# Random-feature attention with a cosine-routed mixture of experts on one core: gate roots and gate work by pairs of token blocks, half sums on TensorE, two GpSimd drains

## Chip, cores and metric

The kernel runs on one core of one Trainium2 chip. The metric is the device time of one execution in microseconds (us); lower is better. TensorE is PE in the profile (PEld is its weight load), VectorE is DVE, ScalarE is ACT, GpSimd is POOL and SyncE is SP; a q behind a name (POOLq, SPq) is the engine's instruction queue.

## The reference, cut to what matters

```python
def phi(x):                                   # omega: 128 x 64
    proj = np.einsum('bhsd,md->bhsm', x, omega)
    return np.concatenate([np.cos(proj), np.sin(proj)], axis=-1) / np.sqrt(m)
q_p, k_p = (phi(q), phi(k))                   # q, k, v: 8 x 8 x 576 x 64
kv = np.einsum('bhsm,bhsd->bhmd', k_p, v)
z = np.sum(k_p, axis=2)
num = np.einsum('bhsm,bhmd->bhsd', q_p, kv)
den = np.einsum('bhsm,bhm->bhs', q_p, z)
...
x = (num / den) as 4608 rows of 512           # 8 heads x 64
xn = x / (np.linalg.norm(x, axis=-1, keepdims=True) + 1e-06)
logits = xn @ en.T / tau                      # en: the 8 normed expert rows
expert_idx = np.argmax(logits, axis=1)
probs = softmax(logits); gate_w = probs[np.arange(N), expert_idx]
for e in range(E):                            # w1: 8 x 512 x 1024, w2: 8 x 1024 x 512
    mask = expert_idx == e
    h = np.maximum(x[mask] @ w1[e], 0.0)
    out[mask] = gate_w[mask, None] * (h @ w2[e])
```

## The kernel before

The work has two stages whose instructions stand in a fixed order written out by hand: each engine runs its own queue in program order, so an instruction that waits holds everything behind it on that engine.

**Attention, 32 steps.** Step n is one pair of heads of one batch (4 pairs, 8 batches; NS is 32). A step projects q and k on TensorE, folds and takes sines and cosines on VectorE and ScalarE, sums the k features on GpSimd (`zsum`, `zsum_tail`, lines 287 to 304), and forms products with v and q on TensorE (lines 312, 333, 348, 379). `norm` divides on VectorE; `to_rows` (GpSimd cast), `sums` (GpSimd, adds a step's unnormed logits to `lacc`) and `squares` (GpSimd, squares the rows in place, line 417; on ScalarE only in the last step) follow one step behind, and `square_sums` (VectorE) three behind. The fp16 rows with their 9 numbers for the gate (8 logits and the sum of squares) go to a buffer in DRAM by SyncE. 32 pieces of expert weights of 512 KB are loaded by GpSimd DMAs, one a step; the set `SOON` (line 1140) says which pieces are issued early in a step, before `norm`, and which at its end.

**Half sums.** The two heads of a step lie in the two halves of the partitions, so a token's logits and sums of squares need both halves added. A group is two batches, and there are four groups. For the logits of the first three and the squares of the first two, ScalarE copies one half beside the other (`other_half`, `square_rows`, line 423) and VectorE adds (`add_halves`, lines 615 and 616, and a reduction at line 443); the rest is added by TensorE matmuls with a stacked identity (`merge`, line 638). The pieces that choose each token's expert are laid into steps 10 to 14 and 18 to 31 (`lay_first`); `rank_here` and `invert_here` are matmuls put after a step's products (`on_pe`).

**Experts, 40 blocks.** Tokens are sorted by expert into blocks of 128; the first 11 blocks (K1) are known before the last attention step, the places of the rest are worked out during blocks 0 to 7 (`route_second`, on VectorE mostly: two comparisons `row_hot` of 128x2304 at line 854, then 36 matmuls `invert` at line 861, then `rows_of_pieces`, which writes the row numbers that gathers 11 to 14 read). Per block j:

- GpSimd gathers the rows of block j+7 (`gather`, line 928, an indirect DMA) into one of four buffers; SyncE turns them (line 977).
- `take_logits` copies the 9 numbers of block j+3 into its slot of `gx` (ScalarE to block 7, VectorE after it), `norm_of` takes the square root on GpSimd as a power (line 449) and adds 1e-6 there (line 450); `gate_shift` (VectorE, lines 984 to 987), `gate_exp` (ScalarE, line 994) and `gate_end` (VectorE, lines 998 and 999) make the gate weight.
- `hidden(j+1)`: 32 matmuls (line 1035), then relu, one half on ScalarE (line 1043), the other on ScalarE to block 7 and on VectorE after it (line 1047). `result(j)`: 8 matmuls (line 1056), the scaled copy on ScalarE (line 1068, below called y(j)), and the scatter to the output by GpSimd (line 1069, an indirect DMA).

In the program's order TensorE does hidden(j+1), then result(j). GpSimd does, for every block from 11 on: square root and addition for block j+3, scatter of block j, gather of block j+7. On VectorE `gate_shift(j+2)` stands ahead of the relu of hidden(j+1). After the 40th block a branch skips three spare blocks, and the kernel ends with drains and semaphores of all engines (lines 1387 and 1431).

Of the kernel before, what the change touches and what calls it, by code (L numbers as in the profile page):

```python
# [11 lines left out]
FP32 = mybir.dt.float32  # L12
# [16 lines left out]
def kernel(  # L29
# [76 lines left out]
    lmax = persist.tile([P, SG], FP32)  # L106
# [23 lines left out]
    pm = persist.tile([P, SG], BF16)  # L130
# [4 lines left out]
    with tc.tile_pool(name="psA", bufs=1, space=PSUM) as psA, tc.tile_pool(  # L135
# [293 lines left out]
        def square_sums(n):  # L429
            b, i = steps[n]  # L430
            if i == 0:
                ssq[b] = pa.tile([P, NCH, 2 * NPAIR], FP32, tag="sq", name="sq", bufs=4)
# [4 lines left out]
        def square_rows(g, par, act):  # L437
            s0 = g * SG
            t = ssq.pop(2 * g + par)
            here = slice(64 * par, 64 * par + 64)  # L440
            there = slice(64 - 64 * par, 128 - 64 * par)
            move("act" if act else "dve", t[here, :, NPAIR:], t[there, :, 0:NPAIR])
            nc.vector.tensor_reduce(
                lsq[here, s0 : s0 + SG, E : E + 1], t[here], axis=AX.X, op=ALU.add
            )
# [140 lines left out]
        def choose_pieces(g, act=True):  # L586
            s0 = g * SG
            lg = lsq[:, s0 : s0 + SG, 0:E]

            def scratch(at, n, own):  # L590
                return ROUTE[:, at : at + n] if act else own

            cp = scratch(0, SG * E, None)
            mx = scratch(72, SG, lmax)
            hit = scratch(81, SG * E, sel.rearrange("p s e -> p (s e)"))
            hit = hit.rearrange("p (s e) -> p s e", e=E)
            top = scratch(153, SG, pm)
            l0, l1 = lg[0:64], lg[64:P]

            def other_half():  # L600
                a0, a1 = lacc[2 * g], lacc[2 * g + 1]
                c0, c1 = l0, l1
                if act:
                    c = cp.rearrange("p (s e) -> p s e", e=E)
                    c0, c1 = c[0:64], c[64:P]
                move("act" if act else "dve", c0, a0[64:P])
                move("act" if act else "dve", c1, a1[0:64])

            def add_halves():
                a0, a1 = lacc.pop(2 * g), lacc.pop(2 * g + 1)  # L610
                c0, c1 = l0, l1
                if act:
                    c = cp.rearrange("p (s e) -> p s e", e=E)
                    c0, c1 = c[0:64], c[64:P]
                nc.vector.tensor_tensor(l0, c0, a0[0:64], ALU.add)
                nc.vector.tensor_tensor(l1, c1, a1[64:P], ALU.add)
# [15 lines left out]
            return [other_half, add_halves, largest, preferred, first_of_them]  # L632

        LATE = ps[:, 6 * 512 + 304 : 7 * 512]

        def merge(at, parts, w):
            for par, t in enumerate(parts):
                nc.tensor.matmul(
                    LATE[64 * par : 64 * par + 64, at : at + w],
                    lhsT=rmat[:, 0, 0, 0:64], rhs=t, start=True, stop=True,  # L640
                )

        def choose_last(g):
            s0 = g * SG
            lg = LATE[:, 0 : SG * E].rearrange("p (s e) -> p s e", e=E)
            nc.scalar.activation(lsq[:, s0 : s0 + SG, 0:E], lg, AF.Copy)
# [500 lines left out]
        for n in range(NS):  # L1147
# [56 lines left out]
            if n > 0:  # L1204
                norm(n - 1)
# [230 lines left out]
```

## Time and profile before

| | us |
|---|---|
| median of 3 runs | 484.4 (482.27 to 495.48) |
| the profiled execution | 485.89 |
| its span, first to last instruction | 484.0 |
| mean granted TensorE clock | 0.986 of full speed |
| last matmul's copy (y of block 39) begins at | 475.12 |

The attention stage takes the first 300 us or so of the span, the expert stage the rest. Rows of the timeline give start, duration, engine, line, operation, what it writes and reads with shapes, a count of merged instructions, and in brackets the idle time before it with what released it.

### The profile page before, as it was taken

What the parts mean: (1) busy time and instruction counts of PE and PEld (TensorE: products, weight loads), DVE (VectorE), ACT (ScalarE), POOL (GpSimd) and SP (SyncE); (2) the same over time, 40 slices, a digit from 0 to 9 for tenths busy, and PEclk for the clock granted to TensorE, in tenths of its full rate; (3) what the DMA queues carried; (4) which work ended last, traced back from release to release, by engine and by line L of the source; (5) the groups of instructions that cost most, each with busy time, mean ns of one, the idle gap of its engine ahead of it and who ended that gap; (6) DMA issues with size and microseconds to landing.
All of it is one profiled execution on the core that took longest, in us unless ns stands there. A gap on an engine that the chain in (4) does not pass through costs nothing. (4 is left out here: it accounts for less than half of the span.)

```text
span 484.0 us, 18932 instructions
## 1 busy us (share of the span) xinstructions
PE 441.2 (91%) x7872; PEld 361.0 (75%) x7872; DVE 321.9 (67%) x731; ACT 342.1 (71%) x457; POOL 389.5 (80%) x500
## 2 busy tenths in 40 slices
PE   5799999999999999988998998799789999999992
PEld 4698988888888888877887887676566666666671
DVE  3589888888888788887898879377643333333340
ACT  6899999999999899887997988455333333333341
POOL 3589999989999889887997979978867777777761
PEclk9999999999999999999999999899899999999997
DMA  6577898888888878957888786447264454454431
GB/s 150 148 157 158 194 165 185 182 178 169 175 182 168 202 156 172 196 127 151 168 184 167 150 177 105 91 115 121 86 128 117 133 128 119 125 139 118 127 96 35
DMA packets 77637, 70.78 MB, mean 146 GB/s; under 512 B 49381, under 2 KB 57573, under 8 KB 77552
## 3 DMA queue, kind: packets, MB, share of 16 engines
q0 software_dynamic: 17920, 31.11, 34.6%
q1 hardware_dynamic: 59328, 38.36, 31.7%
q8 instruction: 65, 1.06, 0.9%
q14 instruction: 20, 0.16, 0.1%
q10 hardware_dynamic: 304, 0.08, 0.1%
HBM read 67.67 MB, written 15.37 MB: 172 GB/s over the span
## 5 line engine op out<-in xcount | busy, mean ns | idle before, releaser
L296 POOL TENSOR_TENSOR zs<-sck 128x512 f32<-128x512 f32 x64 | 82.0, 1282 | 31.2 <-ACT sck L286 28.2
L1056 PE MATMUL ps<-w_sb,late 128*128 x320 | 81.0, 384 | 8.3 <-DVE omT L998 8.3
L1035 PEld LDWEIGHTS <-w_sb 128*128 x1280 | 75.7, 99 | 10.0 <-issue 1.3
L1035 PE MATMUL ps<-kq,w_sb 128*128 128x128 f16 x1280 | 79.2, 221 | 0.7 <-ACT kq L423 0.5
L379 PE MATMUL ps<-kv,siq 128*64 128x73 f32 x1152 | 76.7, 229 | 3.0 <-DVE kv L361 2.8
L379 PE MATMUL ps<-kv,coq 128*64 128x73 f32 x1152 | 75.4, 227 | 0.0
L379 PEld LDWEIGHTS ps<-kv,siq 128*64 128x64 f32 x1152 | 63.5, 136 | 7.5 <-issue 3.3
L379 PEld LDWEIGHTS ps<-kv,coq 128*64 128x64 f32 x1152 | 64.2, 137 | 0.0
L1056 PEld LDWEIGHTS <-late 128*128 128x128 f16 x320 | 29.8, 98 | 42.3 <-DVE late L1047 18.1
L269 DVE SCALAR_TENSOR_TENSOR sck<-sck,ps 128x1152 f32<-128x1152 f32 x32 | 43.3, 1353 | 21.6 <-ACT sck L265 21.6
L985 DVE RECIPROCAL omT<-omT 128x1 f32<-128x1 f32 (+1 forms) x38 | 6.2, 163 | 76.4 <-POOL omT L450 76.4
L221 PEld LDWEIGHTS ps<-omT,kqT 64*128 64x128 f32 x576 | 44.1, 192 | 15.0 <-issue 13.9
L928 POOL DMA_INDIRECT xin_all<-rf_x,prm x40 | 42.7, 1068 | 13.6 <-issue 12.9
L298 POOL TENSOR_TENSOR zs<-zs 128x256 f32<-128x256 f32 x64 | 47.2, 738 | 5.0
L221 PE MATMUL ps<-omT,kqT 64*128 64x128 f32 x576 | 48.6, 282 | 0.6 <-DVE kqT L202 0.6
L276 ACT ACTIVATE sck<-sck 128x1152 f32<-128x1152 f32 x32 | 37.3, 1166 | 12.0 <-DVE sck L269 12.0
L269 DVE SCALAR_TENSOR_TENSOR siq<-siq,ps 128x1152 f32<-128x1152 f32 x32 | 43.0, 1344 | 2.9 <-ACT siq L265 2.9
L280 DVE TENSOR_REDUCE coq<-siq 128x1152 f32<-128x1152 f32 x32 | 43.2, 1350 | 0.1
L184 PE MATMUL ps<-ident,kq 128*128 128x128 f32 x288 | 39.4, 281 | 4.1 <-DVE siq L269 1.7
L265 ACT ACTIVATE siq<-ps 128x1152 f32<-128x1152 f32 x32 | 36.1, 1127 | 9.4 <-PE ps L247 8.3
L312 PE MATMUL ps<-sck,v 64*64 64x128 f32 x1224 | 37.8, 272 | 5.4 <-issue 4.4
L286 ACT ACTIVATE coq<-coq,pio 128x1152 f32<-128x1152 f32 x32 | 39.9, 1248 | 2.5 <-DVE coq L280 2.4
(200 smaller groups left out, 982.6 us busy)
## 6 DMA issues: line engine op xcount, KB each, us to landing
w_sb<-in_moe_w_dram POOLq DMA_DIRECT2D x32, 512.0 KB, 7.4
kq<-in_k_dram SPq DMA_DIRECT2D x64, 144.0 KB, 3.7
kq<-in_q_dram SPq DMA_DIRECT2D x64, 144.0 KB, 3.6
v<-in_v_dram SPq DMA_DIRECT2D x34, 144.0 KB, 4.1
rf_x<-xb SPq DMA_DIRECT2D x32, 144.0 KB, 6.7
xin_all<-in_v_dram SPq DMA_DIRECT2D x30, 144.0 KB, 3.7
xin_all<-rf_x,prm POOLq DMA_INDIRECT x40, 3.4
kq<-xin_all SPq DMA_TRANSPOSE x37, 3.3
```

The costliest lines, as they stand in the source:

```text
L184: nc.tensor.transpose(qreg[:, at : at + P], t[:, j * P : j * P + P], ident)
L221: nc.tensor.matmul(kreg[:, s * P : s * P + P], lhsT=t[r0 : r0 + 64, j * P : j * P + P], rhs=omT[r0 : r0 + 64], start=True, stop=True,)
L269: nc.vector.scalar_tensor_tensor(out=si, in0=si, scalar=CMAGIC, in1=REG[nm], op0=ALU.subtract, op1=ALU.subtract)
L280: nc.vector.tensor_reduce(co.unsqueeze(2), si.unsqueeze(2), axis=AX.X, op=ALU.max, apply_absolute_value=True)
L286: nc.scalar.activation(t, t, AF.Sin, bias=pio2 if which == "co" else 0.0, scale=-TWO_PI * SINSC)
L296: nc.gpsimd.tensor_tensor(z[:, 0:4], t[:, 0:4], t[:, 4:8], ALU.add)
L298: nc.gpsimd.tensor_tensor(r, z[:, 0:2], z[:, 2:4], ALU.add)
L312: nc.tensor.matmul(kreg[64 * half : 64 * half + 64, 512 * hh : 512 * hh + P], lhsT=d["v"][r0 : r0 + 64, c], rhs=d["sck"][r0 : r0 + 64, hal ...
L379: nc.tensor.matmul(nm2[r0 : r0 + 64, a, (c - c0) * W : (c - c0) * W + W], lhsT=ph[:, s * P + r0 : s * P + r0 + 64], rhs=d["kv"][:, half, h ...
L928: ins = nc.gpsimd.indirect_dma_start(out=t, out_offset=None, in_=x_rows[:], in_offset=bass.IndirectOffsetOnAxis(ap=prm[:, j : j + 1], axis=0),
L1035: nc.tensor.matmul(h_ps[:, f * P : f * P + P], lhsT=weights(k), rhs=d["xT"][:, c * P : c * P + P], start=(c == 0), stop=(c == 3),)
L1056: nc.tensor.matmul(y_ps, lhsT=d["hT"][:, c * P : c * P + P], rhs=weights(NW1 + c), start=(c == 0), stop=(c == NW2 - 1),)
```

## The change

- `norm_of` takes the power for two blocks in one GpSimd instruction; the addition of 1e-6 moves into `gate_shift` on VectorE. `gx` has 8 slots, so `take_logits`, `gate_shift` and `gate_end` go by pairs of blocks: logits at even j, `gate_shift` and the exponentials at odd j, `gate_end` at even j. In `route_second` the third block product moves from j = 5 to 4, the two `row_hot` from 6 and 7 to 5 and 6, and `block_experts` behind the gathers.
- All four groups add their half sums by TensorE matmuls; the copies and additions on ScalarE and VectorE go, and one ScalarE copy of 128x72 a group (`kept`) is new.
- Weight pieces 21 and 31 are issued at the end of a step. Gather 0 moves from step 29 to step 30, gathers 1 to 4 stand in step 31 (before: one in step 30, three in 31). The squares of step 29 are taken by ScalarE in step 31.
- `nc.gpsimd.drain()` stands before `result(34)` and `result(37)`.

```diff
         def squares(n):
             x = st[n]["xa"][:, 0:NCH, 0:64]
-            if n < NS - 1:
+            if n not in (NS - 3, NS - 1):
                 nc.gpsimd.tensor_tensor(x, x, x, ALU.mult)
...
+        def gate_slots(j, n=1):
+            a = (j + 1) % 8
+            assert a + n <= 8
+            return gx[:, a : a + n]
 
         def norm_of(j, n=1):
-            r = gx[:, j % 4 : j % 4 + n, E]
+            r = gate_slots(j, n)[:, :, E]
             nc.gpsimd.tensor_tensor(r, r, half1.to_broadcast([P, n]), ALU.pow)
-            nc.gpsimd.tensor_scalar(r, r, 1e-6, None, ALU.add)
...
+        def merge(out, parts):
+            w = out.shape[1]
+            for par, t in enumerate(parts):
+                nc.tensor.matmul(
+                    out[64 * par : 64 * par + 64, 0:w],
+                    lhsT=rmat[:, 0, 0, 0:64], rhs=t, start=True, stop=True,
+                )
...
+            def to_pe():
+                merge_logits(g, at)
+                merge_squares(g, sn)
...
+            def kept():
+                nc.scalar.activation(lsq[:, s0 : s0 + SG, 0:E], lg, AF.Copy)
...
         def gate_shift(j, n=1):
-            g = gx[:, j % 4 : j % 4 + n]
-            nc.vector.tensor_reduce(g[:, :, 10:11], g[:, :, 0:E], axis=AX.X, op=ALU.max)
-            nc.vector.reciprocal(g[:, :, 11], g[:, :, E])
+            g = gate_slots(j, n)
+            nc.vector.tensor_reduce(g[:, :, 9:10], g[:, :, 0:E], axis=AX.X, op=ALU.max)
+            nc.vector.tensor_scalar(g[:, :, E], g[:, :, E], 1e-6, None, ALU.add)
+            nc.vector.reciprocal(g[:, :, 10], g[:, :, E])
...
-            lay(n + 11, [lambda: [piece() for piece in first_rows(r1, K1)], swap], [add])
-            lay(n + 12, [lambda: block_experts(0, K1, False, ar1)], [big])
-            lay(n + 13, [pre], [one])
+            on_pe[n + 10] = lambda: (invert_here(), to_pe2())
+            lay(n + 11, [lambda: [piece() for piece in first_rows(r1, K1)]], [big])
+            lay(n + 12, [], [pre, sq])
+            lay(n + 13, [kept], [one, lambda: block_experts(0, K1, False, Arena(ROUTE[:, 200:]))])
...
-        SOON = {1, 2, 4, 6, 8, 10, 12, 14, 15, 16, 17, 19, 21, 23, 25, 27, 29, 30, 31}
+        SOON = {1, 2, 4, 6, 8, 10, 12, 14, 15, 16, 17, 19, 23, 25, 27, 29, 30}
...
+            if n == NS - 1:
+                squares(n - 2)
...
+            if n == NS - 2:
+                gather(0)
...
-            if NS - 3 <= n < NS:
-                gather(n + 3 - NS)
             if n == NS - 1:
-                gather(3)
-                gather(4)
-            if n > 0:
+                for j in range(1, 5):
+                    gather(j)
+            if n > 0 and n != NS - 2:
                 squares(n - 1)
...
         def taken(t, eng):
-            if t < LAST:
-                take_logits(t, eng)
-                norm_of(t)
+            n = min(2, LAST - t)
+            for a in range(t, t + n):
+                take_logits(a, eng)
+            if n > 0:
+                norm_of(t, n)
...
             if j > FOUND:
-                if j + 1 < LAST:
-                    gate_end(j + 1)
-                if j + 2 < LAST:
-                    gate_shift(j + 2)
+                if even and left > 1:
+                    gate_end(j + 1, min(2, left - 1))
+                if not even and left > 2:
+                    gate_shift(j + 2, min(2, left - 2))
...
+            if j in (LAST - 6, LAST - 3):
+                nc.gpsimd.drain()
             result(j)
-            if 0 < j < LAST - 2:
-                gate_exp(j + 2)
+            if not even:
+                for t in range(j + 2, min(j + 4, LAST)):
+                    gate_exp(t)
```

GpSimd's queue over two blocks of the expert stage, before (omT holds the gate slots, xin_all the gathered rows, late and siq the results y of even and odd blocks):

```order
L449 TENSOR_TENSOR omT<-omT,half_68 128x1
L450 TENSOR_SCALAR omT<-omT 128x1
L1069 DMA out_dram<-siq,prm 4608x512
L928 DMA xin_all<-rf_x,prm 128x530
L449 TENSOR_TENSOR omT<-omT,half_68 128x1
L450 TENSOR_SCALAR omT<-omT 128x1
L1069 DMA out_dram<-late,prm 4608x512
```

The same two blocks now:

```order
L443 TENSOR_TENSOR omT<-omT,half_67 128x2
L1045 DMA out_dram<-late,prm 4608x512
L903 DMA xin_all<-rf_x,prm 128x530
L1045 DMA out_dram<-siq,prm 4608x512
L903 DMA xin_all<-rf_x,prm 128x530
L443 TENSOR_TENSOR omT<-omT,half_67 128x2
```

Two powers and two additions have become one power of two columns; the four transfers stay.

VectorE's queue in blocks 5 to 7 before, from the last block product to the copy that follows the 36 matmuls (ohcoq are the two `row_hot`):

```order
L848 TENSOR_TENSOR ar<-xa,tok_lo 128x36x32
L998 TENSOR_SCALAR omT<-omT 128x1
L999 RECIPROCAL gpos<-omT 128x1
L984 TENSOR_REDUCE omT<-omT 128x1
L985 RECIPROCAL omT<-omT 128x1
L987 TENSOR_SCALAR omT<-omT 128x8
L854 TENSOR_TENSOR ohcoq<-io_p,xa 128x2304
L998 TENSOR_SCALAR omT<-omT 128x1
```

The same place now:

```order
L823 TENSOR_TENSOR ar<-xa,tok_lo 128x36x32
L959 TENSOR_REDUCE omT<-omT 128x2
L960 TENSOR_SCALAR omT<-omT 128x2
L961 RECIPROCAL omT<-omT 128x2
L963 TENSOR_SCALAR omT<-omT 128x8 x2
L829 TENSOR_TENSOR ohcoq<-io_p,xa 128x2304
L974 TENSOR_SCALAR omT<-omT 128x2
L975 RECIPROCAL gpos<-omT 128x2
L829 TENSOR_TENSOR ohcoq<-io_p,xa 128x2304
L959 TENSOR_REDUCE omT<-omT 128x2
```

Between the two comparisons there was a `gate_end` and a `gate_shift`; now there is a `gate_end` alone, and the next `gate_shift` stands behind the second comparison.

GpSimd's queue from the end of step 30's sums to step 31's, before:

```order
L304 TENSOR_TENSOR zs<-zs,sck 128x2x128
L98 DMA w_sb<-in_moe_w_dram 128x4x512
L412 CAST xb<-xa 128x9x64
L459 TENSOR_TENSOR la<-la,xa 128x72
L928 DMA xin_all<-rf_x,prm 128x530
L417 TENSOR_TENSOR xa<-xa 128x9x64
L296 TENSOR_TENSOR zs<-sck 128x512
```

And now:

```order
L303 TENSOR_TENSOR zs<-zs,sck 128x2x128
L903 DMA xin_all<-rf_x,prm 128x530
L411 CAST xb<-xa 128x9x64
L452 TENSOR_TENSOR la<-la,xa 128x72
L98 DMA w_sb<-in_moe_w_dram 128x4x512
L295 TENSOR_TENSOR zs<-sck 128x512
```

The squares (L417) are gone from this place, and the weight piece and the gather have changed sides.

## Rows read from the trace of the kernel before

**Rows 1.** Page, part 1: busy time, share of the span, instructions.

```profile
PE 441.2 (91%) x7872; PEld 361.0 (75%) x7872; DVE 321.9 (67%) x731; ACT 342.1 (71%) x457; POOL 389.5 (80%) x500
```

**Rows 2.** Timeline, ACT, the copies y (L1068) of blocks 2, 6, 7, 9, 37, 39.

```profile
328.55 0.69 ACT L1068 ACTIVATE late<-ps,gpos 128x512 f32<-128x512 f32 x1 [0.97 <-PE ps L1056]
...
342.61 0.69 ACT L1068 ACTIVATE late<-ps,gpos 128x512 f32<-128x512 f32 x1 [0.97 <-PE ps L1056]
351.68 0.69 ACT L1068 ACTIVATE siq<-ps,gpos 128x512 f32<-128x512 f32 x1 [5.08 <-PE ps L1056]
...
358.70 0.69 ACT L1068 ACTIVATE siq<-ps,gpos 128x512 f32<-128x512 f32 x1 [1.96 <-PE ps L1056]
...
469.88 0.69 ACT L1068 ACTIVATE siq<-ps,gpos 128x512 f32<-128x512 f32 x1 [1.96 <-PE ps L1056]
...
475.12 0.69 ACT L1068 ACTIVATE siq<-ps,gpos 128x512 f32<-128x512 f32 x1 [1.04 <-PE ps L1056]
```

**Rows 3.** Timeline, POOL, one block of the expert stage (blocks 32 and 33).

```profile
457.12 1.09 POOL L1069 DMA_INDIRECT out_dram<-late,prm  x1 [0.56 <-issue]
458.52 1.06 POOL L928 DMA_INDIRECT xin_all<-rf_x,prm  x1 [0.30 <-issue]
459.59 0.60 POOL L449 TENSOR_TENSOR omT<-omT,half 128x1 f32<-128x1 f32 x1
460.28 0.23 POOL L450 TENSOR_SCALAR omT<-omT 128x1 f32<-128x1 f32 x1
461.07 1.08 POOL L1069 DMA_INDIRECT out_dram<-siq,prm  x1 [0.56 <-issue]
```

**Rows 4.** Waits: engine and line, waited for; us in total, times, longest.

```profile
DVE omT L985 <- POOL omT L450: 76.4, 33, 5.0
...
PEld L1056 <- DVE late L1047: 18.1, 26, 1.4
```

**Rows 5.** Timeline, DVE, POOL and PE, 339.5 to 348 us.

```profile
339.64 0.16 DVE L985 RECIPROCAL omT<-omT 128x1 f32<-128x1 f32 x1 [2.75 <-POOL omT L450]
...
340.04 2.55 DVE L854 TENSOR_TENSOR ohcoq<-io_p,xa 128x2304 bf16<-128x2304 bf16 x1
340.20 3.37 POOL L1069 DMA_INDIRECT out_dram<-late,prm  x1 [0.59 <-DVE omT L987]
...
344.54 0.16 DVE L985 RECIPROCAL omT<-omT 128x1 f32<-128x1 f32 x1 [1.63 <-POOL omT L450]
...
347.55 0.96 PE L861 MATMUL ps<-ar,ohcoq 128*128 128x64 bf16 x18 [2.67 <-DVE omT L998]
```

**Rows 6.** Instructions of the queues at the end: count, ns min/median/max, first and last start.

```profile
L1431 POOLq DRAIN  x3: 46/103/5219, 477.9 to 483.6; - x3
L1431 SPq DRAIN  x3: 7/13/130, 480.0 to 483.7; - x3
```

**Rows 7.** Groups by form, the power: count, busy us, mean ns.

```profile
L449 POOL TENSOR_TENSOR omT<-omT,half 128x1 f32<-128x1 f32 x37 | 22.2, 601 | 0.9
...
L449 POOL TENSOR_TENSOR omT<-omT,half 128x3 f32<-128x3 f32 x1 | 0.9, 912 | 0.0
```

**Rows 8.** Page, part 6: DMA issues with their count and median us to landing.

```profile
xin_all<-rf_x,prm POOLq DMA_INDIRECT x40, 3.4
```

**Rows 9.** Timeline of single places of the attention stage and its end.

```profile
220.97 0.45 PE L312 MATMUL ps<-sck,v 64*64 64x128 f32 x8 [1.51 <-issue]
...
280.09 0.49 ACT L423 ACTIVATE ps<-la 64x72 f32<-64x72 f32 x2 [1.54 <-PE ps L333]
...
301.67 1.16 POOL L417 TENSOR_TENSOR xa<-xa 128x576 f32<-128x576 f32 x1
...
308.67 0.61 PE L348 MATMUL ps<-ones,zs 64*128 64x1 f32 x8 [1.75 <-POOL zs L304]
...
318.59 0.35 PE L638 MATMUL ps<-la,rmat 128*64 128x72 f32 x4
```

**Rows 10.** Busy us (and count) of PE, PEld, DVE, ACT and POOL, PE's granted clock, DMA share, GB/s; 60 to 80 us.

```profile
60.00:80.00 20.00, 20.00 (x448) 17.89 (x443) 16.14 (x25) 18.69 (x19) 18.70 (x23) 1.00 0.86 169
```

More of the change, by code (lines that the diff above doesn't have):

```diff
@@ new lines, with merge_logits, merge_squares @@
+        SQ, SN = SG * E, SG * NPAIR
+        def merge(out, parts):
[5 more added lines that the diff above has]
+                )
+        def merge_logits(g, at):
+            merge(at[:, 0:SQ], [lacc.pop(2 * g + par).rearrange("p c e -> p (c e)") for par in range(2)])
+        def merge_squares(g, at):
+            merge(at[:, 0:SN], [ssq.pop(2 * g + par).rearrange("p c i -> p (c i)") for par in range(2)])
@@ L618, in largest, with choose_pieces, three @@
+        def choose_pieces(g, at):
+            s0 = g * SG
+            def three(w):
+                return w.rearrange("p (s e) -> p s e", e=E)
+            lg = three(at[:, 0:SQ])
+            mx = lmax
+            hit = three(at[:, SQ : 2 * SQ])
+            top = at[:, 2 * SQ : 2 * SQ + SG]
+            sn = at[:, 2 * SQ + SG : 2 * SQ + SG + SN]
+            def to_pe():
+                merge_logits(g, at)
+                merge_squares(g, sn)
             def largest():
@@ L959, in take_logits @@
         def take_logits(j, eng):
[L960 removed]
+            move(eng, gate_slots(j)[:, 0, 0:NG], xin[j][:, D:XW].bitcast(FP32))
         def turn_x(j, eng, k=None, logits=True):
@@ L1112, in lay_first @@
             ) = first_pieces(r1, S1, K1, oh1, ar1)
-            lay(n, [swap], [add])
-            lay(n + 1, [big], [pre])
-            lay(n + 2, [one], [scan])
-            lay(n + 3, [full, squares_in(1, 0)], [ahead])
-            lay(n + 4, [limits, squares_in(1, 1)], [late])
+            lay(n + 1, [big, sq], [pre])
+            lay(n + 2, [one, kept], [scan])
+            on_pe[n + 2] = rank_here
+            lay(n + 3, [full], [ahead])
+            lay(n + 4, [limits], [late])
             lay(n + 5, [start, shift], [own])
@@ L1248 @@
         to_rows(NS - 1)
+        for j in range(3, 5):
+            take_logits(j, "act")
+        norm_of(3, 2)
         turn_rows(3)
@@ L1279, in own_arena @@
             )
[L1281 to L1291 removed]
+        _, big, pre, one, kept, sq = choose_pieces(NGRP - 1, LATE)
         def route_second(j):
             if j == 0:
[L1295 removed]
+                merge_logits(NGRP - 1, LATE)
                 gate_end(0, 3)
[L1297 removed]
+                kept()
+                big()
+                pre()
+                one()
                 squares(NS - 1)
@@ L1300, in route_second @@
             elif j == 1:
-                gate_shift(3)
+                gate_shift(3, 2)
                 square_sums(NS - 2)
@@ L1369 @@
                 turn_rows(t)
-            if j != FOUND + 1:
+            if even and j > 0 and j != FOUND + 1:
                 taken(j + 3, eng)
```

157 lines of the change are left out of this document (42 added, 115 removed).

## The prediction

> **What bounds the kernel now.** I read the page's first part, then the timeline by engine, then the waits, then the last instructions. TensorE is busy for 91% of the span and GpSimd for 80% [rows 1], but an average says little here, so I went by stages. In the expert stage the copy y(j) on ScalarE marks each block's end, and the reader should look at the distance between such rows. From block 2 to block 6 it is (342.61 - 328.55) / 4 = 3.515 us [rows 2]: that is TensorE's own pace, since in these blocks the next 32 matmuls follow the last 8 at once. From block 9 to block 37 it is (469.88 - 358.70) / 28 = 3.971 us [rows 2]. What paces those blocks is GpSimd: scatter 1.09, gap 0.30, gather 1.06, power 0.60, gap 0.09, addition 0.23, gap 0.56, and the next scatter begins 461.07 - 457.12 = 3.95 us after the last one [rows 3]. Nothing is left over in that sum. The wait list agrees by another way: VectorE waits 76.4 us for the additions, and, since the relu stands behind `gate_shift` in its queue, TensorE's weight loads for the last four matmuls wait 18.1 us for that relu [rows 4]. So GpSimd holds VectorE, and VectorE holds TensorE.
>
> Between blocks 6 and 7 there are 9.07 us [rows 2]. TensorE stood still for 2.67 us before the last 18 of the 36 matmuls [rows 5], because VectorE's two comparisons of 2.55 us came late: it waited 2.75 and 1.63 us for GpSimd ahead of them, and GpSimd was held in a scatter of 3.37 us [rows 5].
>
> At the end the last drain of GpSimd runs from 477.9 for 5.22 us, to 483.1, while SyncE, which waits for the last scatter's landing, is already free at 480.0 [rows 6].
>
> **The change part by part.** Times are those of the profiled execution, 485.89 us around a span of 484.0; it lies 1.5 us above the median of 484.4.
>
> *1. Roots by pairs.* Per two blocks GpSimd loses one power and two additions. The power of two columns does not stand in the trace: one column takes 0.60 and three take 0.91 us [rows 7], so I take 0.76 and keep 0.60 and 1.20 (two single ones) as ends. A pair then costs 2 x 1.09 + 2 x 1.06 for the transfers, three gaps of 0.30 between them, 0.76, and a gap of 0.56 ahead of the scatter [rows 3]: 6.5 us, or 3.26 a block. TensorE needs 3.515, so TensorE becomes the bound. If all four gaps were 0.56 and the power 1.20, it would be 7.74, or 3.87 a block.
>
> What is queued behind the power? The scatter of block j. The power waits for the two logit copies, which stand on VectorE behind the relu of hidden(j+1). That relu can start about 2.6 us before y(j) ends (8 matmuls and the copy), and takes 0.7 and the copies 0.3, so the power can start about 1.1 us before y(j) ends; with 0.76 and 0.56 the scatter begins 0.2 to 0.3 us late. The second scatter of the pair has 3.5 us to make this good. The four y buffers take up such a lag, so it reaches nobody. VectorE gets its five operations of `gate_shift` in one go every second block, about 1.1 us; they must wait for the power, and end before the next relu is due. Gain: 28 x (3.971 - 3.515) = 12.8 us, at most that, and down to 28 x (3.971 - 3.87) = 2.8 by the other end.
>
> *2. The way to block 7.* VectorE's waits of 2.75 and 1.63 us went to the roots of blocks 7 and 8. Now one power serves both, it stands a scatter earlier in GpSimd's queue, and the two comparisons follow each other with a `gate_end` between. Both come earlier by more than the 2.67 us that TensorE lost, so TensorE finds both ready. Then y(7) follows y(6) by one block of 3.515 and 36 matmuls. These took 0.96 for the last 18, begun on a rested TensorE [rows 5]; I take 1.5 for all. 9.07 - 5.0 = 4.1 us are gained. Ends: 1 us, if the second comparison still ends last, and 4.5.
>
> What is late next are gathers 11 to 14, which wait for the row numbers behind the 36 matmuls. They move with y(7), and hidden(11) comes four blocks after hidden(7), about 9 us behind the matmuls, with 3.4 us for a landing [rows 8] and some 5 us for four gathers and a turn: near, but covered.
>
> Here a rule speaks against the change. The rows show a scatter stretched from 1.09 to 3.37 us beside a comparison of 2.55 [rows 3, 5]. The Trainium skill (SBUF — State Buffer, "SBUF: two separate sides") says that GpSimd cannot write descriptors while VectorE holds their shared ports in its fast mode; the trace agrees. With the comparisons closer together, two stretched scatters stand ahead of the power for blocks 9 and 10, and `gate_shift(9)` stands ahead of the row numbers. By that rule part 2 could come to nothing; it is the second rival.
>
> *3. From attention to experts.* TensorE waits 1.75 us for the last k sums of GpSimd [rows 9]. The squares of 1.16 us, a step's length ahead of them in the same queue [rows 9], leave this place for ScalarE, which waits there for VectorE anyway; the gather that leaves step 31's start is replaced by gather 0, but step 29's is gone too. So the k sums end 1.2 us earlier. What is late next is kvT on VectorE and ScalarE's copies of the logits, which wait for gathers 1 and 2; these are issued when they were, since the squares saved are spent on one more gather. I take 1.1 us, from 0 to 1.5.
>
> *4. The drains.* The last drain runs 3.1 us beyond the landing at 480.0; the two drains after it took 0.05 and 0.10 us [rows 6]. A drain with little before it is thus short, and I read the 5.22 us as work on what has piled up since the start (112 transfers, or 0.047 us each). Then a drain before `result(34)` does 106 of these, some 5 us, while scatters wait in four y buffers, and the last one has three left: it ends with the landing. Gain 3.1 us. The trace cannot show this, so the ends are: nothing, or 1 us lost if the drains hold the root of block 39, which stands between them, until VectorE's relu is late. The cover of the first drain is GpSimd's slack once the gathers have ended (block 32): two scatters and a power in 7 us.
>
> *5. Half sums.* In the attention stage TensorE is busy without a gap and ScalarE for 18.7 of 20 us [rows 10]; ScalarE loses six copies of 64x72 (0.49 for two [rows 9]) and four of 64x36, 2.4 us, and gets three of 0.24. The wait of 1.54 us at 280.09 [rows 9], where a copy stood ahead of the step's own work, goes, though TensorE holds ScalarE some 0.6 us later there. TensorE gets twelve small matmuls, at 0.35 for two of 72 columns with their two weights [rows 9] about 0.5 us a group, in steps where it is as full as ScalarE: 1.5 us back. Net 1 us gained.
>
> *6. Weight pieces.* Two pieces move by a few us. There are gaps of 1.5 us on TensorE in which it waits for nothing that is recorded [rows 9]; I count the move at nothing, and parts 5 and 6 together at -3 to +3.5, two such gaps more or less.
> The Trainium skill (Runtime: NRT & Kernel Launch, "Instruction fetch mechanics") has the fetch of code mostly hidden. If those gaps are code fetch, the row disagrees; by the page the move is worth 0, by the row up to 1.5 for each gap that it removes, and both lie within the range above.
>
> **Sum.** 12.8 + 4.1 + 1.1 + 3.1 + 1.0 = 22.1 us. 485.9 - 22.1 = 463.8, and against the median, 1.5 less, 462.3. I forecast 463.
>
> **The rivals.**
> - *The drains bring nothing* (the 3.1 us are a fixed end of any last drain). For it: one drain of this size is all there is to go by. Against it: the two short ones. 463 + 3.1 = 466. Chance 0.2.
> - *The way to block 7 stays as long*, because the root of blocks 9 and 10 comes late behind stretched scatters. For it: the scatter of 3.37 us. Against: two of these end with the second comparison, and the 36 matmuls end 1.5 us or more after it. 463 + 4 = 467. Chance 0.08.
> - *GpSimd stays the pace* at 3.87 a block: 463 + 10 = 473. For it: part 1's margin is only 0.5 us a pair. Chance 0.08.
> - *Slower than before: pairs make VectorE wait for gathers.* At even j VectorE copies the logits of blocks j+3 and j+4, and the second gather was issued three blocks ago, no longer four. Behind that copy stands the next `gate_shift` and relu. From the gather's issue to the copy there are 3 x 3.5 less 1.4 (scatter and gap) less about 1.1: 8 us, against 3.4 to landing [rows 8]. The wait begins at 8 us, and the 22 us are used up when each of 15 pairs waits 1.5 us, that is at landings of 9.5 us: 486 and more. Against: nothing in the expert stage lands that late. Chance 0.03.
> - *No net change*, by several of the small ends together: 0.02.
>
> My forecast has 0.59. A run of this kernel can be told from no change at about 2%, 9.7 us, so faster means under 474.7: the forecast, the first two rivals and half of the third, 0.9; same 0.07; slower 0.03. Range: the good ends of parts 2, 3, 5 and 6 take 0.4, 0.4 and 2.5 us off, 460, and the runs of before spread by 2 to 3 us about their middle: 457. At the other side the third rival gives 473, and 474 with the 1 us that the drains may lose. 457 to 474.
>
> **What would show it.** Right: y rows 3.5 us apart from block 8 to 37, with VectorE's wait for the power gone as a cause of TensorE's; y(7) about 5 us after y(6); a last drain that ends with the last landing; a drain of some 5 us before scatter 34 that nobody waits for. Wrong: a last drain still of 5 us; blocks at 3.7 us or more with GpSimd without gaps; a wait of VectorE for `xin_all`; attention steps longer by code gaps.

## The result and the profile after

The changed kernel takes 464.35 us in the median of 4 runs (463.07 to 469.57), the kernel before, beside it, 484.67 (482.27 to 495.48): a ratio of 0.961, with a 95% interval of 0.952 to 0.969. The forecast was 463, in a range of 457 to 474. The profiled span is 461.3 us, 22.7 less than before. (Three profiled executions below, those of half sums alone, weight pieces alone and no drains, were disturbed in the attention stage; of them only the expert stage and the end are read.)

The page's first part answers to [rows 1]. GpSimd has lost 22.6 us of work, TensorE fills 96% of the span:

```profile
PE 440.7 (96%) x7892; PEld 365.5 (79%) x7892; DVE 320.5 (69%) x671; ACT 338.5 (73%) x451; POOL 366.9 (80%) x443
```

The timeline of ScalarE has the copies y (now L1044) of blocks 6, 7, 8, 9, 37 and 39, to be laid beside [rows 2]:

```profile
339.92 0.69 ACT L1044 ACTIVATE late<-ps,gpos 128x512 f32<-128x512 f32 x1 [0.93 <-PE ps L1032]
...
344.48 0.69 ACT L1044 ACTIVATE siq<-ps,gpos 128x512 f32<-128x512 f32 x1 [2.12 <-PE ps L1032]
...
347.99 0.69 ACT L1044 ACTIVATE late<-ps,gpos 128x512 f32<-128x512 f32 x1 [1.97 <-PE ps L1032]
...
351.50 0.69 ACT L1044 ACTIVATE siq<-ps,gpos 128x512 f32<-128x512 f32 x1 [1.96 <-PE ps L1032]
...
449.93 0.69 ACT L1044 ACTIVATE siq<-ps,gpos 128x512 f32<-128x512 f32 x1 [1.96 <-PE ps L1032]
...
455.17 0.69 ACT L1044 ACTIVATE siq<-ps,gpos 128x512 f32<-128x512 f32 x1 [1.04 <-PE ps L1032]
```

From block 6 to 7 there are 4.56 us (9.07 before), from 9 to 37 98.43, or 3.515 a block (111.18, 3.971). The blocks now run at the pace at which blocks 2 to 6 always ran. From the last copy to the end there are 461.3 - 455.17 = 6.1 us (8.9).

The whole 22.7 us, by the same marks: 12.75 in blocks 9 to 37, 4.5 from block 6 to 7, 2.75 at the end, 5.05 in attention steps 1 to 31 (from one step's first ScalarE copy of 128x1152, L264, to the other's: 276.74 and 271.69), 0.45 from there to the first y copy; less 2.5 before step 1 and 0.3 in blocks 0 to 6. (How the attention stage's share divides depends on the copy that is taken as the mark; part 5 below says by how much.)

GpSimd in the timeline, a pair of blocks (answers to [rows 3]):

```profile
380.63 1.01 POOL L1045 DMA_INDIRECT out_dram<-siq,prm  x1 [1.12 <-ACT omT L970]
381.94 1.03 POOL L903 DMA_INDIRECT xin_all<-rf_x,prm  x1 [0.30 <-issue]
383.00 0.73 POOL L443 TENSOR_TENSOR omT<-omT,half 128x2 f32<-128x2 f32 x1
384.16 1.04 POOL L1045 DMA_INDIRECT out_dram<-late,prm  x1 [0.42 <-ACT late L1044]
385.50 1.04 POOL L903 DMA_INDIRECT xin_all<-rf_x,prm  x1 [0.30 <-issue]
387.65 1.01 POOL L1045 DMA_INDIRECT out_dram<-siq,prm  x1 [1.11 <-ACT omT L970]
```

Both scatters now wait for ScalarE, 1.12 and 0.42 us: GpSimd is no longer the pace. The waits say the same (answers to [rows 4]): ScalarE's y copies wait for TensorE, and VectorE's wait for GpSimd's root, 76.4 us before, is 26.0; TensorE's wait for the relu has gone from 18.1 to 0.3 us.

```profile
ACT siq L1044 <- PE ps L1032: 36.4, 20, 2.1
ACT late L1044 <- PE ps L1032: 33.2, 19, 2.0
DVE omT L974 <- ACT omT L970: 27.9, 15, 2.1
DVE omT L960 <- POOL omT L443: 26.0, 17, 3.8
...
PEld L1032 <- DVE late L1023: 0.3, 1, 0.3
```

On the way to block 7 (timeline, VectorE, GpSimd and TensorE; answers to [rows 5]) both comparisons are through by 340.8 and the 36 matmuls run in one piece:

```profile
334.73 0.17 DVE L960 TENSOR_SCALAR omT<-omT 128x2 f32<-128x2 f32 x1 [1.62 <-POOL omT L443]
334.89 1.05 POOL L1045 DMA_INDIRECT out_dram<-late,prm  x1 [0.20 <-issue]
...
338.29 2.54 DVE L829 TENSOR_TENSOR ohcoq<-io_p,xa 128x2304 bf16<-128x2304 bf16 x1
339.07 2.34 POOL L443 TENSOR_TENSOR omT<-omT,half 128x2 f32<-128x2 f32 x1
341.50 1.21 PE L836 MATMUL ps<-ar,ohcoq 128*128 128x64 bf16 x36
342.55 1.89 PE L1032 MATMUL ps<-w_sb,late 128*128 x8
```

More went than the wait of 2.67 us. In the kernel before, TensorE was busy for 0.38 of the 3 us ahead of the last 18 matmuls, and behind them the granted clock was 0.58 and 0.57, in part at the lower of its two levels (1.2 of 2.4 GHz); the 8 matmuls of result(7) took 3.31 us there and take 1.89 now. In the changed kernel TensorE has no pause at this place and the clock stays at 1.00. Of the kernel before, one row of TensorE and the windows (us, TensorE's busy time and count, granted clock, DMA share, GB/s):

```profile
348.32 3.31 PE L1056 MATMUL ps<-w_sb,late 128*128 x8
```

```profile
344.50:347.50 3.00, 0.38 (x13) 1.00 0.10 40
347.50:349.50 2.00, 1.95 (x21) 0.58 0.29 98
349.50:351.50 2.00, 2.00 (x7) 0.57 0.12 39
```

The queues' drains (count, ns min/median/max, first and last start; answers to [rows 6]): the two added ones, then those at the end.

```profile
L1349 POOLq DRAIN  x2: 3819/4666/5513, 438.5 to 447.1; - x2
...
L1404 POOLq DRAIN  x3: 46/103/2704, 457.3 to 461.0; - x3
L1404 SPq DRAIN  x3: 7/7/13, 460.4 to 460.7; - x3
```

The added drains stand where nobody waits: the y copies around them stay 3.51 us apart. The last one takes 2.70 us, not 5.22, and ends at 460.0, ahead of SyncE, which waits for the last landing and is free at 460.4; before, it ended 3.1 us behind SyncE.

### The profile page after: what moved, and what is told of

Its sections match the earlier page's. It is cut to its first block, busy times and chain, and to the rows that moved or that the text cites. A ratio compares the mean times of both kernels' runs of the same rounds, so it can differ in the third digit from the quotient of the medians.

```text
span 461.3 us, 18852 instructions
## 1 busy us (share of the span) xinstructions
PE 440.7 (96%) x7892; PEld 365.5 (79%) x7892; DVE 320.5 (69%) x671; ACT 338.5 (73%) x451; POOL 366.9 (80%) x443
## 4 chain that ended last, share of the span: by engine, by line
PE 87%; DVE 5%; issue 2%; ACT 2%; POOL 1%; DMA 1%; ACTq 0%; POOLq 0%; DVEq 0%
PE ps L378 16%; PE ps L311 15%; PE ps L1011 14%; PE ps L1032 14%; PE ps L237 8%; PE ps L183 7%; PE ps L220 7%; PE ps L332 3%; PE ps L347 2%; POOL out_dram L1045 1%; ACT sck L285 1%; DVE sq L432 1%; ACT sck L264 1%; DVE sck L268 1%; DMA w_sb<-in_omega_dram 1%
## 5 line engine op out<-in xcount | busy, mean ns | idle before, releaser
L1011 PEld LDWEIGHTS <-w_sb 128*128 x1280 | 74.7, 98 | 9.4 <-issue 0.6
L378 PE MATMUL ps<-kv,siq 128*64 128x73 f32 x1152 | 76.4, 229 | 2.2 <-DVE kv L360 1.8
L1011 PE MATMUL ps<-kq,w_sb 128*128 128x128 f16 x1280 | 78.0, 219 | 0.5 <-ACT kq L422 0.5
L1032 PE MATMUL ps<-w_sb,late 128*128 x320 | 75.5, 379 | 0.0
L220 PEld LDWEIGHTS ps<-omT,kqT 64*128 64x128 f32 x576 | 45.7, 197 | 15.9 <-issue 14.6
L220 PE MATMUL ps<-omT,kqT 64*128 64x128 f32 x576 | 50.2, 287 | 0.6 <-DVE kqT L201 0.6
L275 ACT ACTIVATE sck<-sck 128x1152 f32<-128x1152 f32 x32 | 37.3, 1167 | 11.4 <-DVE sck L268 11.4
L264 ACT ACTIVATE siq<-ps 128x1152 f32<-128x1152 f32 x32 | 36.1, 1129 | 10.9 <-PE ps L246 9.5
L311 PE MATMUL ps<-sck,v 64*64 64x128 f32 x1224 | 40.6, 287 | 3.5 <-issue 2.1
L311 PEld LDWEIGHTS ps<-sck,v 64*64 64x64 f32 x1224 | 36.5, 142 | 6.5 <-issue 4.1
L1044 ACT ACTIVATE siq<-ps,gpos 128x512 f32<-128x512 f32 x20 | 13.7, 687 | 36.4 <-PE ps L1032 36.4
```

Of the source, the lines that this page charges most:

```text
L220: nc.tensor.matmul(kreg[:, s * P : s * P + P], lhsT=t[r0 : r0 + 64, j * P : j * P + P], rhs=omT[r0 : r0 + 64], start=True, stop=True,)
L264: nc.scalar.activation(si, REG[nm], AF.Copy, bias=CMAGIC, scale=1.0)
L311: nc.tensor.matmul(kreg[64 * half : 64 * half + 64, 512 * hh : 512 * hh + P], lhsT=d["v"][r0 : r0 + 64, c], rhs=d["sck"][r0 : r0 + 64, hal ...
L378: nc.tensor.matmul(nm2[r0 : r0 + 64, a, (c - c0) * W : (c - c0) * W + W], lhsT=ph[:, s * P + r0 : s * P + r0 + 64], rhs=d["kv"][:, half, h ...
L1011: nc.tensor.matmul(h_ps[:, f * P : f * P + P], lhsT=weights(k), rhs=d["xT"][:, c * P : c * P + P], start=(c == 0), stop=(c == 3),)
L1032: nc.tensor.matmul(y_ps, lhsT=d["hT"][:, c * P : c * P + P], rhs=weights(NW1 + c), start=(c == 0), stop=(c == NW2 - 1),)
```

## The experiments

Runs 1 to 4 ran on one chip, 5 to 8 on a second, 9 to 12 on a third; the kernel before, run beside them, had medians of 490.83, 486.57 and 488.97 us. Ratios are to it, with the 95% interval. Only the lines that carry an edit are shown.

**1 and 9. Gate work by pairs alone, twice.**

```diff
 # from the kernel before: gate_slots, norm_of, gate_shift, gate_end, taken
 # and the route_second order of the change
-            nc.gpsimd.tensor_scalar(r, r, 1e-6, None, ALU.add)
+            nc.vector.tensor_scalar(g[:, :, E], g[:, :, E], 1e-6, None, ALU.add)
```

> The kernel before with the gate work by pairs alone (roots of two blocks in one GpSimd instruction, the 1e-6 addition on VectorE, shifts and ends of the gates by pairs); half sums, weight pieces and the end as before. Theory: this is parts 1 and 2 of the prediction. From y copy to y copy 3.5 to 3.55 us over blocks 9 to 37 (98 to 99.5 us instead of 111.2), from the y copy of block 6 to that of block 7 about 4.6 to 5.0 us instead of 9.07, first y copy and end as before: 484.0 - 12.8 - 4.2 = about 467 us. Rival (the half sums of all groups, which also shorten the list of choice work, are needed for the way to block 7): the step from block 6 to 7 stays over 7 us, and the kernel ends near 471 us.

Measured: 482.63 us, ratio 0.985 (0.978 to 0.991). Block 6 to 7 took 4.56 us, as expected, but blocks 7 to 9 took 10.87 instead of 7.02 and blocks 9 to 37 105.7 us, with y copies alternating at about 2.7 and 4.9 us. The timeline of that execution, VectorE, GpSimd, TensorE and ScalarE:

```profile
401.87 0.69 DVE L1052 TENSOR_SCALAR late<-ps 128x512 f16<-128x512 f32 x1 [3.26 <-PE ps L1061]
...
402.48 0.24 DVE L425 COPY omT<-xin_all 128x9 f32<-128x9 f32 x2
...
402.80 0.72 POOL L454 TENSOR_TENSOR omT<-omT,half 128x2 f32<-128x2 f32 x1 [1.70 <-DVE omT L425]
...
404.36 0.68 DVE L1052 TENSOR_SCALAR late<-ps 128x512 f16<-128x512 f32 x1
...
409.47 1.05 PE L1040 MATMUL ps<-kq,w_sb 128*128 128x128 f16 x16 [0.35 <-issue]
...
409.55 0.69 DVE L1052 TENSOR_SCALAR late<-ps 128x512 f16<-128x512 f32 x1 [3.27 <-PE ps L1040]
```

GpSimd has time to spare: its root waits 1.70 us for the copies of the logits, which stand behind a relu that waited 3.26 us; addition and shifts follow, and the next relu comes right behind them. In the changed kernel the root follows the gather without a wait. No engine is full here (TensorE, the busiest, works 36.3 of 38.3 us); the pair goes round a loop of VectorE, GpSimd and TensorE in 7.65 us. Is this loop what pairs do without the other parts?

> The kernel of the first experiment a second time (gate work by pairs alone, from the kernel before), beside the three below. There blocks 7 to 9 took 10.9 us instead of 7.0 and blocks 9 to 37 105.7 us with y copies alternating at 2.7 and 4.9 us; the changed kernel and three of its variants, on other chips, kept 3.51. Theory (a rhythm: once a delay around blocks 7 to 9 has put VectorE's relu behind the gate chain, the pair takes 7.65 us and stays so; the delay came with that chip or execution): this time 98.4 to 99.5 us over blocks 9 to 37 and 467 us or so. Rival (half sums or weight pieces are needed for the pace): again 105 us or more.

Measured the second time, on another chip: 468.71 us, ratio 0.953 (0.943 to 0.963); blocks 7 to 9 in 7.02, 9 to 37 in 98.41, y 3.51 to 3.52 us apart. The same kernel has two rhythms. The delay around blocks 7 to 9 (10.9 to 12.0 us) stood in all four traces of the first chip, three of which don't have the pairs, and in none of the other ten. In run 1 TensorE paused four times there within one pass of `hidden`, 2.2 us in all, with no releaser in the trace, and the 8 matmuls behind the pauses took 2.88 us instead of 1.89. What made the delay stays open, as does why TensorE pauses in the slow rhythm.

**2. The drains alone.**

```diff
+            if j in (LAST - 6, LAST - 3,):
+                nc.gpsimd.drain()
             result(j)
```

> The kernel before with the two drains of GpSimd in the late blocks alone. GpSimd sets the pace here (3.97 us a block), so this is the test of drains where they are not hidden. Theory (the drain at the end takes long because over a hundred software transfers have piled up since the last one): the two drains in the last blocks take about 5 and 4 us of GpSimd's time in the middle of its work, each of which delays the scatters and gathers behind it and so TensorE by up to that much; the last drain goes from 5.2 to 2.7 us and the end shortens by 2.7 us; together between 482 (waits covered by the blocks already gathered) and 489 us (not covered). Rival (the last drain only waits for the last scatter to land and cannot be shortened): it stays at 5.2 us, and the kernel is at 484 us or longer by the drains.

Measured: 491.48 us, ratio 1.003 (0.996 to 1.010), so nothing in all. The last drain fell to 1.84 us and the end to 5.1, but the first added drain held the root of one block: VectorE waited 6.16 us for its addition and TensorE 3.02 for the relu behind it, and y of blocks 36 and 37 stand 7.54 us apart instead of 3.51. (The second row below names L998, which stands right behind that relu on VectorE.) With another 0.5 us in the next block this is more than the 3.8 us that the end gains.

```profile
475.10 0.16 DVE L985 RECIPROCAL omT<-omT 128x1 f32<-128x1 f32 x1 [6.16 <-POOL omT L450]
```

```profile
476.36 1.86 PE L1056 MATMUL ps<-w_sb,late 128*128 x4 [3.02 <-DVE omT L998]
```

The drains need slack on GpSimd, here the slack that the relief of GpSimd makes.

**3 and 4. Half sums alone; weight pieces, gathers and squares alone.** The edits are those of the change.

> The kernel before with the half sums of all groups added on TensorE alone (choice and squares of all groups from PSUM), weight pieces, gate work and end as before. Theory of the prediction: about 1 us net, from fewer ScalarE copies before the turn of the attention steps, so 483 us. Rival (the 5.05 us by which attention steps 1 to 31 came out shorter are due to this part): whole attention steps 1 to 31 at 272 us instead of 276.7 and the kernel at 479 to 480 us. Other rival (they are due to the weight pieces or to the code place of TensorE's instructions): 484 us here.

Measured: 490.33 us, ratio 0.998 (0.991 to 1.006). Alone the half sums bring nothing that can be seen, and the 1 us that was forecast is too little to be seen in this interval; block 6 to 7 stays at 8.9 us, so that gain is not theirs.

> The kernel before with the other weight piece places, gathers and the squares of step 29 on ScalarE alone; half sums, gate work and end as before. Theory of the prediction: nothing, 484 us within 1 us. Rival (the 5.05 us of attention steps 1 to 31 come from here, as three pauses of 1.3 to 1.6 us of TensorE with no releaser go away): those pauses are absent and the kernel is at 479 to 480 us.

Measured: 488.46 us, ratio 0.986 (0.977 to 0.995), its runs spread from 482.45 to 498.49: inconclusive against either number, though the interval leans to the rival's. Block 6 to 7 took 7.4 us here, where the kernel before and runs 2 and 3 took 8.9 to 9.1; why is open.

**5 and 6. The changed kernel again, and without its drains** (the two lines of run 2 removed).

> The changed kernel unchanged, as a control beside the next three on one chip. In the first set the gate work by pairs alone kept a block at 3.78 us in the middle stretch, not 3.52, with TensorE pausing 0.35 to 0.5 us in the middle of one pass in each pair. Theory (what the other parts add is the steady pace): here 3.51 to 3.52 us a block again, 464 us. Rival (the pace of pairs has two rhythms and which one it falls into depends on the delays around blocks 7 to 9 of that execution): 3.75 to 3.85 us a block can come here too, and the kernel is then near 472 us.

Measured: 464.33 us, ratio 0.964 (0.953 to 0.975); blocks 9 to 37 in 98.41 us, attention steps 1 to 31 in 271.80. Step 1 began at 22.6 as in the kernel before, so the 2.5 us lost ahead of it in the first pair of profiles belong to that execution; its granted clock was 0.50 from 20 to 22 us and 0.65 from 22 to 24, that of the kernel before 1.00.

> The changed kernel without the two drains of GpSimd in the late blocks. Theory of the prediction (the last drain takes long because 112 software transfers have piled up): the last drain is 5.2 us again instead of 2.7 and the kernel 2.5 to 3 us longer than the changed one, 467 us. Rival (the drain at the end waits for the last scatter alone): no difference.

Measured: 466.64 us, ratio 0.965 (0.955 to 0.974). 2.3 us more than the control in the median, less than the spread of either; but the row shows the step itself. The last drain is back:

```profile
L1402 POOLq DRAIN  x3: 46/103/5215, 467.3 to 473.1; - x3
```

From the last y copy to the end: 8.9 to 9.2 us where the drains are absent (before, runs 1, 6, 9, 11), 4.6 to 6.1 us where they are present and hidden (after, runs 5, 7, 8, 12).

**7, 8 and 10. Which half of the root's relief does it?**

```diff
 # run 7: the addition back on GpSimd, behind the root of the pair
+            nc.gpsimd.tensor_scalar(r, r, 1e-6, None, ALU.add)
 # run 8: the root by single blocks, the addition on VectorE
+            for a in range(j, j + n):
+                r = gate_slots(a)[:, :, E]
+                nc.gpsimd.tensor_tensor(r, r, half1.to_broadcast([P, 1]), ALU.pow)
 # run 10: as run 8, with the addition behind each root on GpSimd
```

> The changed kernel with the 1e-6 addition back on GpSimd (for the pair, behind the root, as it was behind each root before). GpSimd's work for a pair is 2 scatters, 2 gathers and one root (6.2 to 6.5 us with the gaps) and becomes about 6.9 us, against the 7.03 us that TensorE needs for two blocks. Theory (only the pace of the slowest engine counts): no change, 464 us. Rival (GpSimd at 98 percent can't take up its waits for y copies and gate sums): a block takes up to 3.8 us and the kernel is up to 8 us longer. Either way VectorE waits longer for the root.

> The changed kernel with the roots one block at a time (two power instructions of one column each where one of two columns stands), the addition on VectorE as in the changed kernel. This is the amortisation alone. GpSimd's work for a pair grows by one power and its gap, about 0.6 to 0.9 us, to 7.0 to 7.2 us. Theory (pairs of roots are what takes GpSimd below TensorE): a block at 3.5 to 3.65 us, the kernel 0 to 4 us longer than the changed one. Rival (the addition taken off GpSimd was enough, pairs are not needed): the same time as the changed kernel.

Measured: run 7 467.09 us, ratio 0.968 (0.957 to 0.978), blocks 9 to 37 in 99.42; run 8 467.48 us, ratio 0.962 (0.947 to 0.977), 99.11. In both all blocks but one stand 3.51 us apart; the one that does not, right after the switch at block 9, takes 4.56 and 4.25. So either half alone is nearly enough.

> The changed kernel with roots and additions one block at a time on GpSimd (a power and an addition of one column for each block, as before the change), the rest of the gate work by pairs, half sums, weight pieces and drains as changed. One half of the relief alone was enough for 3.51 us a block (99.4 us over blocks 9 to 37 with the addition back on GpSimd for the pair, 99.1 with single roots, 98.4 with both reliefs). Theory (GpSimd's queue is the pace once it passes 7.03 us a pair): its pair is 7.9 us again, a block takes 3.9 to 3.97 us, blocks 9 to 37 take 109 to 111 us, and the kernel is 10 to 13 us longer than the changed one, 475 to 477 us. Rival (the order by pairs is what took away the wait, not GpSimd's work): under 102 us over blocks 9 to 37.

Measured: 479.15 us, ratio 0.982 (0.973 to 0.991); blocks 9 to 37 in 108.8 us, 3.886 a block. Of these 7.22 us are the one step behind the switch at block 9; from there to block 34 y copies stand 3.51 and about 4.1 us apart in turn, 7.6 a pair or 3.8 a block, a little under the 3.9 to 3.97 that was expected. From the last y copy to the end there are 8.3 us although the drains are there: with GpSimd as the pace the second drain ends at 468.4, behind the last y copy (467.1), and the last three scatters stand behind it. The timelines of GpSimd, run 7 and then run 10:

```profile
383.03 0.73 POOL L443 TENSOR_TENSOR omT<-omT,half 128x2 f32<-128x2 f32 x1
383.85 0.23 POOL L444 TENSOR_SCALAR omT<-omT 128x2 f32<-128x2 f32 x1
384.64 1.06 POOL L1045 DMA_INDIRECT out_dram<-late,prm  x1 [0.56 <-issue]
...
389.76 0.73 POOL L443 TENSOR_TENSOR omT<-omT,half 128x2 f32<-128x2 f32 x1
```

```profile
392.97 0.59 POOL L444 TENSOR_TENSOR omT<-omT,half 128x1 f32<-128x1 f32 x1
393.66 0.23 POOL L445 TENSOR_SCALAR omT<-omT 128x1 f32<-128x1 f32 x1
393.97 0.57 POOL L444 TENSOR_TENSOR omT<-omT,half 128x1 f32<-128x1 f32 x1
394.62 0.22 POOL L445 TENSOR_SCALAR omT<-omT 128x1 f32<-128x1 f32 x1
395.41 1.12 POOL L1046 DMA_INDIRECT out_dram<-late,prm  x1 [0.56 <-issue]
...
399.52 1.04 POOL L905 DMA_INDIRECT xin_all<-rf_x,prm  x1 [0.31 <-issue]
```

Run 7's pair takes 389.76 - 383.03 = 6.73 us with no wait, under the 7.03 of TensorE; run 10's takes 399.52 + 1.04 - 392.97 = 7.6, over it, and that is the pace of its y copies. In these kernels the gate's order is the same, and the pace goes with the larger of the two sums. It is not the only thing that can hold the pace: in run 1 a pair took 7.65 us while GpSimd had time to spare.

**11. Pairs and half sums, without drains and with the old places.**

> The changed kernel without the drains and with the weight pieces, gathers and squares of step 29 at their places of before: gate work by pairs and half sums alone. Against the kernel without drains (y copies 9 to 37 in 98.4 us, end 9.0 us after the last y copy) only the weight pieces differ. Theory (the weight pieces are worth nothing): 466 to 468 us, attention steps 9 to 31 in the same pattern as the changed kernel (a step of 9.7 us third from there, none over 10.6 but for pauses of TensorE). Rival (the places are what holds the pace of the blocks or the shorter steps): 3 us or more above the kernel without drains, or blocks 9 to 37 over 102 us.

Measured: 474.85 us in the median of four runs that spread from 469.5 to 482.65, so no verdict on its time. The profiled execution lies at a span of 467.7 with blocks 9 to 37 in 98.43; its steps have the changed kernel's pattern but for the last two, 11.4 and 10.5 us against 10.0 to 10.5 and 8.8 with the new places, and TensorE pauses 1.75 us without a releaser in the first of the two and 1.47 in the last. One execution can't say whether the places or the pauses did it: open.

**12. The drains at blocks 12 and 24.**

```diff
-            if j in (LAST - 6, LAST - 3):
+            if j in (12, 24):
```

> The changed kernel with the two drains at blocks 12 and 24 instead of 34 and 37. At block 12 some 65 software transfers have gone since the start, to block 24 some 24 more, to the end another 23; the last two transfers before a drain need up to 3.5 us to land, which no drain can undercut. Theory of the prediction (0.047 us a transfer): the first drain 3.0 to 3.5 us, the second no more than the landing, the last 1.4 to 2.7 us as with late drains. Rival (the first drain in the work costs a fixed 5 us, the later ones little): 5.0 to 5.5 us at block 12. The kernel 464 us if the waits are hidden by the gathers of seven blocks ahead.

Measured: 461.17 us in a single run. The drain before block 12 and GpSimd's work around it:

```profile
L1349 POOLq DRAIN  x1: 4536/4536/4536, 359.6 to 359.6; - x1
```

```profile
360.95 0.73 POOL L443 TENSOR_TENSOR omT<-omT,half 128x2 f32<-128x2 f32 x1
365.04 1.04 POOL L1045 DMA_INDIRECT out_dram<-late,prm  x1 [3.36 <-ACT omT L970]
```

A drain's row begins when the queue reaches it, while GpSimd still works. Its 4.54 us lie between the two numbers expected, 3.0 to 3.5 and 5.0 to 5.5, but it stood alone only from the root's end, 361.68, to 364.14: 2.46 us, 4.3 after the last gather's issue, so even that may be the landing. The second drain, 24 transfers later, stood alone for 2.3 us. The drain before block 34, read the same way, stood alone for 4.75 us in all six profiles that have it (the changed kernel, runs 2, 5, 7, 8 and 10), whether it came at 436 or at 467 us. After some 63 transfers a drain thus costs at most 2.5 us, after 106 4.75, after 112 5.2 (the last one, in every kernel without drains). A fixed 5 us for the first one is out, and the time since the start does not set the price. It rises with what has piled up; that it does so in proportion, 0.047 us a transfer, is not shown, since 63 and 24 transfers cost nearly the same here.

## Why the prediction was right, by its own steps

- **Part 1, roots by pairs, 12.8 us: 12.75.** Pairs alone give 12.77 (run 9). The step's bound was right, and the rival by which GpSimd stays the pace, at 3.87 a block, has its place where both reliefs are undone: run 10 shows 3.8 in its steady pairs, by other terms than the rival's (two additions, not four gaps of 0.56). GpSimd's pair was put at 6.5 us; it is nearer 6.0 (7.02 in the rows above, less waits of 1.12 and 0.42 where gaps of 0.30 and 0.20 would stand). The root of two columns took 0.73 against 0.76. The overestimate is mostly the gap: I took 0.56 ahead of the scatter, but that gap belongs to the addition (0.56 behind it in runs 7 and 10) and falls to 0.20 behind a power. What the prediction did not see is that the margin was wide enough for half of the edit.
- **Part 2, the way to block 7, 4.1 us: 4.5.** It comes with the gate work by pairs (4.56 and 4.57 us in runs 1 and 9, 8.9 with half sums alone). The prediction named 2.67 us of it, the wait; the rest of its 4.1 stood in the difference 9.07 - 5.0 without a cause. The rows above give one: at the lower clock behind that wait result(7) lost 1.4 us and the last 18 matmuls, which took 0.96 us where the first 18 took 0.69, lost 0.3. The 36 matmuls, put at 1.5 us, took 1.21. The rival by the shared ports fell on its outcome, not on its premise: the root was stretched to 2.34 us beside the second comparison, yet VectorE waited only 0.53 us for it, behind the second comparison, and the 36 matmuls had both.
- **Part 3, from attention to experts, 1.1 us: 0.45 in the pair of profiles.** Mis-sized there; over executions this stretch is 21.7 to 22.1 us without the new half sums and places (before, runs 1, 2, 9) and 20.2 to 21.3 with them (after, runs 5, 7, 8, 12; 21.8 in run 10), so some 0.8. The wait from which the step set out, 1.75 us for the k sums, is gone. But TensorE now waits 0.68 us for VectorE shortly before, and its pause without a releaser in the same place took 1.75 us instead of 1.31. The reason given, the squares that leave, was not needed: run 11 has them at their old place and no wait for the k sums there either. What else brought the k sums forward is open. The new wait, in the changed kernel:

```profile
301.23 0.38 PE L941 MATMUL ps<-ident,xin_all 128*128 128x128 f16 x4 [0.68 <-DVE eblk L882]
```

- **Part 4, the drains, 3.1 us: 2.75, and 2.8 to 4.6 by the spread of the ends above.** The rival that they bring nothing fell with runs 6 and 12. Their cover was named as GpSimd's slack after the last gather; run 2 shows what they cost without it, all that they bring, and run 12 that in the changed kernel there is slack enough while the gathers still go. The price taken, 0.047 us a transfer, met the 4.75 us after 106 (5.0); after 63 and fewer it is not shown.
- **Parts 5 and 6, 1.0 us net, -3 to 3.5: 5.05 in this pair.** By the marks above the forecast was outrun. What outran it are the pauses of TensorE without a releaser, of which the prediction allowed two more or less. In steps 1 to 31 the kernel before has three of them, 4.4 us together, and the changed kernel none of 1 us or more. Over the profiles there are two or three of 1.0 to 2.1 us in every old one (before, runs 1, 2, 9) and none to two, of up to 2.2 us, in the new ones (after, runs 5, 7, 8, 10, 12), and with them steps 1 to 31 of the one new attention stage spread over 7 us (271.7 to 278.8). Whether the change removes pauses or the pair was lucky is argued, not shown; the middle of the profiles, 276.7 against 272.5, speaks for some 3 us. What is left without pauses, the shortest of each of steps 1 to 31, adds up to 271.6 us in the four old profiles and to 270.6 in the six new ones, the 1.0 us that was worked out. But this hangs on the mark. From each step's copy to sck instead (L264 too, the k half) the two sums are 270.4 and 270.3, the pair gives 2.64 us for these steps instead of 5.05 and 1.46 for part 3 instead of 0.45, and part 3 is some 1.8 us over the executions. By either mark part 3 and the regular part come to 1.8 or 1.9 us together, of 2.1 forecast; how they divide is not shown. The surplus of 5.05 us and the 2.5 us lost before step 1 nearly cancelled, and that was luck: it is why the sum met the time so closely.

## What to carry to other kernels

Where one engine paces a loop, add up its queue with the gaps and compare with the next engine's pace: once it is under, more relief buys little (1 us here, 98.4 against 99.1 and 99.4), and the cheapest edit that gets it under is enough. A drain of GpSimd's software transfers took longer behind 106 of them than behind 63 or fewer, and two of them shortened the one at the end, so put one where the engine has slack and not where it is the pace. When a wait of TensorE goes, look at the granted clock behind it as well: on the way to block 7 the slower matmuls held 1.7 us beside the 2.67 of the wait. Repeat a run on another chip before a slow pace is put down to an edit.

## What the runs showed of the hardware

- A small operation on GpSimd costs more than its row: the addition of 0.23 us also lengthens the gap to the next transfer from 0.20 to 0.56 us (runs 7 and 10 against the changed kernel).
- VectorE's wide comparison stretches GpSimd's arithmetic too, not only its transfers: the root of 0.73 us took 2.34 beside it and ended 0.58 us behind it, and 2.30 to 2.42 us in runs 1, 5, 6, 9, 11 and 12. The Trainium skill (SBUF — State Buffer, "SBUF: two separate sides") has the ports that the two engines share as a lock, held for a whole instruction, also between a VectorE operation with two SBUF inputs and a GpSimd operation that reads SBUF. The row agrees with that case; the prediction had drawn on the section for the writing of descriptors alone.
- A pause of TensorE can cost more than its length. In run 9 one of 1.73 us was followed by a granted clock of 0.83 and then 0.50 (the lower level, 1.2 GHz), and two steps took 3.2 us longer together than the shortest of the old profiles; one of 1.51 us in the kernel before [rows 9] left the clock at 1.00. Run 9's row, then its windows (us, TensorE's busy time and count, granted clock, DMA share, GB/s):

```profile
202.53 0.44 PE L312 MATMUL ps<-sck,v 64*64 64x128 f32 x6 [1.73 <-issue]
```

```profile
200.00:202.50 2.50, 0.81 (x26) 1.00 0.97 232
202.50:205.00 2.50, 2.46 (x22) 0.83 0.96 183
205.00:208.00 3.00, 3.00 (x28) 0.50 1.06 232
```
